# Letting forced background work finish the tasks that already hold buffers, and moving layer 2's units forward, in a four-layer attention kernel

## The chip, the cores and the metric

The kernel runs on one core of a Trainium2 chip. The metric is the time of one execution on the device, in microseconds (us), as the median of several runs.

## The reference

```python
x = x + A(layernorm(x), A_wqkv, A_wo)   # layer 0, sliding window: 0 <= q - k < 256
x = x + B(layernorm(x), B_wqkv, B_wo)   # layer 1, full attention
x = x + A(layernorm(x), A_wqkv, A_wo)   # layer 2, sliding window
x = x + B(layernorm(x), B_wqkv, B_wo)   # layer 3, full attention
# x is 2048 x 640 bf16, 32 heads of 20; attention is not causal in B
# A, B: softmax(q k^T / sqrt(20)) v, then @ wo
```

## The kernel before

The queries are cut into NC = 4 chunks of 512, the heads into G = 8 groups of four. A **unit** is (layer, chunk, group). A full unit of layers 1 and 3 scores 512 queries against all 2048 keys, for four heads; a unit of layers 0 and 2 only needs the window. All units stand in one fixed list, and their score matmuls, exponentials and value matmuls are emitted in this order, one tile of up to 3 x 512 columns at a time. Everything else (layernorm, projections of q, k and v, output products) is **background work**: Python generators, each with a `need`, the index of the unit that wants its result. After each tile `pump` lets the background emit a little, up to a credit. Where a unit's data isn't ready, `require` forces the background on, and no scores are emitted meanwhile; each pass of its loop is called a turn below. Units (1,0,0) to (1,0,2) are halved: part "a" takes the keys of chunks 0 to 2, part "b" those of chunk 3. While layer 0's units and the "a" parts run, every other tile is only 2 x 512 columns wide, and background matmuls have two banks of PSUM (the memory that TensorE writes to); after that they have one. The code is shortened where a comment says so.

```python
def choose(blocked, limit=1 << 30):
    if state["held"] is not None:        # inside an accumulation group
        return state["held"]
    for t in tails:
        if t.wake <= state["tick"]:
            return t
    if not blocked:
        for t in todo:                   # in order of need
            if t.need > limit:
                break
            if t.wake <= state["tick"]:
                return t
    return None

def require(what):
    n = 0
    while what not in ready:
        n += 1                           # ... (an assert)
        t = choose(False, state["unit"] if n < 400 else 1 << 30)
        if t is None:
            state["tick"] += 1
            continue
        state["credit"] = max(state["credit"] - advance(t), -1.0)

cap = {"qa": 3, "ka": 18, "va": 10, "xnT": 5, "kt": 3, "vt": 3, "qt": 4, "ln": 1, "w": 2, "vs": 2}

def room(*tags):
    while any(live[t] >= cap[t] for t in tags):
        yield ("wait", 1)
    for t in tags:
        live[t] += 1

def t_qk_full(key, l, c, g):             # one head group's k and q of a chunk
    # ... (waits for the normalised input)
    wt = yield from take_w(key, l)       # room("w"), then the weights' load
    for n, dst in ((1, k_d[l][:, g, c * C : (c + 1) * C]), (0, q_d[l][:, c, g, :])):
        yield from project(wt, n, xnT[l, c], staged)     # five matmuls, an eviction
        nc.sync.dma_start(out=dst, in_=staging.pop())    # to memory; the unit loads it back
    live["w"] -= 1

# the order of the units (after layer 0's; the rest of layer 3 follows)
units += [Unit(1, 0, g, "a") for g in range(3)]                    # keys of chunks 0 to 2
units += [Unit(1, 0, g, "b" if g < 3 else None) for g in range(G)] # "b": keys of chunk 3
for c in range(1, NC + 1):
    small = deque(Unit(2, c - 1, g) for g in range(G))
    for g in range(G):
        units.append(Unit(1, c, g) if c < NC else Unit(3, 0, g, "a"))
        for _ in range(((0, 0, 1, 1, 2, 2, 2, 0) if c < NC else (0, 0, 2, 3, 3, 0, 0, 0))[g]):
            units.append(small.popleft())

pump(1.2 if cur[0][0].l == 0 else 0.6)   # the credit of one tile
```

The softmax here doesn't subtract the row's maximum and nothing guards it: scores larger than these inputs give would overflow.

Of the kernel before, what the change touches and what calls it, by code (L numbers as in the profile page):

```python
# [23 lines left out]
NC = S // C  # L24
# [7 lines left out]
def kernel(  # L32
# [119 lines left out]
    state = {"tick": 0, "held": None, "credit": 0.0, "early": True, "act": True, "unit": 0}  # L152

    class Task:
# [3 lines left out]

        def __init__(self, name, gen, need):
            self.name, self.gen, self.need, self.wake = name, gen, need, 0  # L160
            Task.count += 1
            self.key = (need, Task.count)

# [9 lines left out]
    def drop(task):  # L173
        (tails if task in tails else todo).remove(task)

    def advance(task):
        try:
            kind, n = next(task.gen)
        except StopIteration:
            drop(task)  # L180
            state["held"] = None
            return 0.0
        state["held"] = task if kind == "hold" else None
        if kind == "wait":
            task.wake = state["tick"] + n
            return 0.0
        return n

    def choose(blocked, limit=1 << 30):
        if state["held"] is not None:  # L190
# [3 lines that stand above are left out]
                return t  # L194
        if not blocked:
            for t in todo:
                if t.need > limit:
                    break
                if t.wake <= state["tick"]:
                    return t  # L200
        return None

    def pump(credit):
        state["credit"] = min(state["credit"] + credit, 1.0)
        while True:
            t = choose(state["credit"] <= 0.0)
            if t is None:
                break
            state["credit"] -= advance(t)
# [17 lines left out]
    def end_early():  # L227
        while mfree[5][0] == 1 << 30:
            advance(state["held"])
        del mfree[5]  # L230
        state["early"] = False
# [4 lines that stand above are left out]
            n += 1  # L236
            assert n < 100000, what
# [5 lines that stand above are left out]
# [5 lines left out]
    def room(*tags):  # L248
        while any(live[t] >= cap[t] for t in tags):
            yield ("wait", 1)  # L250
        for t in tags:
            live[t] += 1

    users = {}

# [35 lines left out]
    def take_w(key, l):  # L291
        yield from room("w")
        order = worder[l]
        i = next(n for n, e in enumerate(order) if e[0] == key)
        if key not in wtiles:
            wtiles[key] = get_w(*order[i][1:])
            if not order[i][3]:
                yield ("wait", 4)
        i = next(n for n, e in enumerate(order) if e[0] == key)
        order.pop(i)  # L300
        wt = wtiles.pop(key)
        if i < len(order) and not any(e[0] in wtiles for e in order):
            wtiles[order[i][0]] = get_w(*order[i][1:])
        return wt
# [35 lines left out]
    def t_ln(l, c):  # L340
        while ("x", l, c) not in ready:
            yield ("wait", 1)
        yield from room("xnT", "ln")
        users[l, c] = 10 if l == 1 else 9
        mv = mvs.pop((l, c))
# [35 lines left out]
    def t_v(l, c, halves):  # L381
# [9 lines left out]
        for i in range(4):  # L391
            if windowed:
                yield from room("va")
                va[c, i] = vap.tile([P, H, VW], BF16, name="va", tag="va")
                nc.gpsimd.memset(va[c, i][:, :, DH : DH + 1], 1.0)
# [176 lines left out]
    for c in range(1, NC + 1):  # L572
        small = deque(Unit(2, c - 1, g) for g in range(G))
        for g in range(G):
            units.append(Unit(1, c, g) if c < NC else Unit(3, 0, g, "a"))
            for _ in range(((0, 0, 1, 1, 2, 2, 2, 0) if c < NC else (0, 0, 2, 3, 3, 0, 0, 0))[g]):
                units.append(small.popleft())
    units += [Unit(3, 0, g, "b") for g in range(G)]
    units += [Unit(3, c, g) for c in range(1, NC) for g in range(G)]
# [304 lines left out]
```

## Time and profile before

| | before |
|---|---|
| median | 2606.18 us (2598.14 to 2611.42, 3 runs) |
| ScalarE busy | 2261.0 us, 87% of the span |
| TensorE busy | 2122.9 us, 81% |
| ScalarE's exponentials waited for scores | 261.8 us, of which one wait 104.7 us and one 35.6 us |
| TensorE's granted clock, mean (share of full speed) | 0.712 |

How to read it: the share of ScalarE is an average over stages. In the filled stages it is busy all the time; what can be won is in the stretches where its exponentials (line 803) wait for score matmuls (line 789). Two waits make up more than half of that.

### The profile page before, as it was taken

What the parts mean: (1) busy time and instruction counts of PE and PEld (TensorE: products, weight loads), DVE (VectorE), ACT (ScalarE), POOL (GpSimd) and SP (SyncE); (2) the same over time, 40 slices, a digit from 0 to 9 for tenths busy, and PEclk for the clock granted to TensorE, in tenths of its full rate; (3) what the DMA queues carried; (4) which work ended last, traced back from release to release, by engine and by line L of the source; (5) the groups of instructions that cost most, each with busy time, mean ns of one, the idle gap of its engine ahead of it and who ended that gap; (6) DMA issues with size and microseconds to landing.
All of it is one profiled execution on the core that took longest, in us unless ns stands there. A gap on an engine that the chain in (4) does not pass through costs nothing.

```text
span 2605.6 us, 37526 instructions
## 1 busy us (share of the span) xinstructions
PE 2122.9 (81%) x15424; PEld 744.8 (29%) x15424; DVE 852.6 (33%) x1925; ACT 2261.0 (87%) x1831; POOL 48.1 (2%) x113
## 2 busy tenths in 40 slices
PE   6889867977888788878888777889887787778777
PEld 3334432322322233322332233323222222222222
DVE  6687833310222233424443343453310011001101
ACT  6778703999999899999999976899999999999996
POOL 2000000000000000000000000000000000000000
PEclk9899987955675669865897668968765565556555
DMA  5112142411211012300222013212310111001100
GB/s 170 61 52 61 50 143 86 127 48 46 59 42 46 16 44 82 104 31 31 72 90 82 1 24 100 88 37 61 111 55 31 31 41 47 31 31 41 47 16 11
DMA packets 92892, 153.03 MB, mean 59 GB/s; under 512 B 8880, under 2 KB 59056, under 8 KB 92720
## 3 DMA queue, kind: packets, MB, share of 16 engines
q1 hardware_dynamic: 92720, 150.64, 18.8%
q8 instruction: 120, 1.97, 0.3%
q14 instruction: 52, 0.43, 0.1%
HBM read 120.46 MB, written 30.15 MB: 58 GB/s over the span
## 4 chain that ended last, share of the span: by engine, by line
ACT 49%; PE 28%; issue 12%; DVE 8%; DMA 2%; SPq 0%; POOL 0%; ACTq 0%; DVEq 0%
ACT pt L803 48%; PE ps L317 10%; PE ps L789 6%; PE ps L481 4%; PE ps L842 4%; PE ps L404 3%; DVE pt L827 2%; DMA wqk<-wqk_d 1%; DVE oT L667 1%; PE ps L368 1%; DVE st L265 1%; DVE qa L265 1%; PE ps L713 1%; DVE x_sb L489 0%; DVE xn L359 0%
## 5 line engine op out<-in xcount | busy, mean ns | idle before, releaser
L803 ACT ACTIVATE pt<-ps 128x1536 bf16<-128x1536 f32 (+1 forms) x1688 | 2194.9, 1562 | 277.7 <-PE ps L789 261.8
L789 PE MATMUL ps<-qt,kt 32*128 32x512 bf16 x4096 | 736.2, 519 | 306.9 <-ACT pt L803 285.0
L842 PE MATMUL ps<-pt,vt 128*21 128x512 bf16 x4096 | 549.3, 522 | 3.7 <-DVE oT L667 1.5
L789 PEld LDWEIGHTS <-kt 32*128 32x128 bf16 x4096 | 209.9, 96 | 793.0 <-issue 770.2
L317 PE MATMUL ps<-xnT,wqk 128*128 128x512 bf16 x1280 | 367.1, 428 | 43.2 <-DMA wqk<-wqk_d 30.6
L827 DVE TENSOR_TENSOR pt<-pt,masks 128x1024 bf16<-128x1024 bf16 (+4 forms) x403 | 239.9, 625 | 242.7 <-ACT pt L803 242.5
L667 DVE CAST oT<-ps 128x512 bf16<-128x512 f32 x117 | 80.2, 685 | 574.8 <-PE ps L842 574.4
L842 PEld LDWEIGHTS <-vt 128*21 128x21 bf16 x4096 | 106.3, 92 | 336.8 <-issue 332.2
L481 PE MATMUL ps<-wop,on 128*128 128x320 bf16 x1024 | 182.6, 327 | 11.1 <-DVE x_sb L489 5.1
L317 PEld LDWEIGHTS <-wqk 128*128 128x128 bf16 x1280 | 120.5, 105 | 223.3 <-issue 107.5
L789 PE MATMUL ps<-qa,ka 32*128 32x256 bf16 (+2 forms) x1408 | 136.5, 322 | 34.0 <-ACT pt L803 30.6
L265 DVE CAST st<-ps 128x512 bf16<-128x512 f32 x119 | 82.3, 691 | 189.9 <-PE ps L317 188.9
L489 DVE TENSOR_TENSOR x_sb<-x_sb,ps 128x320 bf16<-128x320 bf16 x128 | 61.9, 484 | 189.9 <-PE ps L481 187.3
L404 PE MATMUL ps<-wv,xnT 128*128 128x320 bf16 x640 | 114.1, 318 | 10.7 <-DVE vs L265 5.6
L481 PEld LDWEIGHTS <-on 128*128 128x128 bf16 x1024 | 99.0, 105 | 81.4 <-issue 39.4
L717 DVE TENSOR_TENSOR on<-oT,ps 128x512 bf16<-128x512 bf16 x128 | 87.5, 684 | 94.7 <-PE ps L713 94.4
L842 PE MATMUL ps<-pt,va 128*21 128x384 bf16 (+2 forms) x1408 | 89.7, 324 | 18.5 <-DVE oT L667 18.2
L694 DVE RECIPROCAL rz<-ps 128x16 f32<-128x16 f32 x128 | 32.7, 256 | 169.0 <-PE ps L689 159.8
L404 PEld LDWEIGHTS <-xnT 128*128 128x128 bf16 x640 | 60.3, 102 | 53.6 <-issue 30.3
L789 PEld LDWEIGHTS <-ka 32*128 32x128 bf16 x1408 | 40.2, 96 | 122.7 <-issue 115.8
L713 PE MATMUL ps<-rT,spread 32*128 32x128 bf16 x512 | 65.6, 264 | 2.3 <-DVE rT L706 1.5
L368 PE MATMUL ps<-ident,xn 128*128 128x128 bf16 x320 | 35.7, 258 | 31.5 <-DVE xn L359 28.8
(50 smaller groups left out, 647.8 us busy)
## 6 DMA issues: line engine op xcount, KB each, us to landing
wqk<-wqk_d SPq DMA_DIRECT2D x120, 320.0 KB
kt<-k_d SPq DMA_DIRECT2D x53, 512.0 KB
vt<-v_d SPq DMA_DIRECT2D x53, 336.0 KB
qt<-q_d SPq DMA_DIRECT2D x75, 128.0 KB
k_d<-st SPq DMA_DIRECT2D x64, 128.0 KB
q_d<-st SPq DMA_DIRECT2D x64, 128.0 KB
v_d<-vs SPq DMA_DIRECT2D x16, 336.0 KB
wqk_d<-wqk SPq DMA_DIRECT2D x16, 320.0 KB
```

The source lines that it names most:

```text
L265: nc.vector.tensor_copy(out=out_, in_=in_)
L317: nc.tensor.matmul(pq, lhsT=wt[:, n, dc, :], rhs=xt[:, dc, :], start=(dc == 0), stop=(dc == KD - 1),)
L404: nc.tensor.matmul(pv, lhsT=xt[:, dc, i * P : (i + 1) * P], rhs=wv_sb[l % 2][:, dc, h * HD : (h + 1) * HD], start=(dc == 0), stop=(dc == K ...
L481: nc.tensor.matmul(yp, lhsT=on[:, g, qb * P : (qb + 1) * P], rhs=wop[:, g, i * HD : (i + 1) * HD], start=(g == 0), stop=(g == G - 1),)
L489: nc.vector.tensor_tensor(out=xv, in0=xv, in1=yp, op=ALU.add)
L667: nc.vector.tensor_copy(out=oT[:], in_=op)
L713: nc.tensor.matmul(zb[:, qb * P : (qb + 1) * P], lhsT=spread4[:, qb, :], rhs=rT[:], start=True, stop=True,)
L717: nc.vector.tensor_tensor(out=on[:, g, :], in0=oT[:], in1=zb, op=ALU.mult)
L789: nc.tensor.matmul(sp[:, i, col * P : (col + qn) * P], lhsT=u.k(kc, j), rhs=u.q(j, q0, qn), start=True, stop=True,)
L803: nc.scalar.activation(out=pt[:, i:k, b0 * P :], in_=sp[:, i:k, b0 * P :], func=ACT.Exp, scale=SCALE,)
L827: nc.vector.tensor_tensor(out=pt_[:, i:k, b0 * P :], in0=pt_[:, i:k, b0 * P :], in1=mv_, op=ALU.mult,)
L842: nc.tensor.matmul(op[32 * j : 32 * j + VW, q0 * P : (q0 + qn) * P], lhsT=u.v(kc, j), rhs=pt[:, i, col * P : (col + qn) * P], start=(first ...
```

## The change

The intent: a task that has taken a buffer must be able to finish when a forced task needs that buffer, and layer 2's small units should end earlier, so that layer 3's first inputs are made behind layer 1's last units.

```diff
@@ class Task
             self.name, self.gen, self.need, self.wake = name, gen, need, 0
+            self.holds = False
@@ advance
+        state["running"] = task
@@ choose
             for t in todo:
-                if t.need > limit:
-                    break
-                if t.wake <= state["tick"]:
+                if t.wake <= state["tick"] and (t.need <= limit or t.holds):
                     return t
@@ room
             live[t] += 1
+        state["running"].holds = True
@@ order of the units
-            for _ in range(((0, 0, 1, 1, 2, 2, 2, 0) if c < NC else (0, 0, 2, 3, 3, 0, 0, 0))[g]):
+            for _ in range(((0, 0, 2, 2, 2, 2, 0, 0) if c < NC else (0, 0, 2, 3, 3, 0, 0, 0))[g]):
```

The number and the shapes of the instructions stay the same; only their order changes. I call the first four hunks part 1 and the last one part 2. (The changed kernel has one line more, so its exponential is line 804 and its score matmul line 790.)

## The prediction

> **What bounds the kernel now.** I first read the page's share of busy time and the granted clock, then who waited for whom on ScalarE, and then cut the span where ScalarE's work changes its rhythm.
>
> ```profile
> PE 2122.9 (81%) x15424; PEld 744.8 (29%) x15424; DVE 852.6 (33%) x1925; ACT 2261.0 (87%) x1831; POOL 48.1 (2%) x113
> ...
> ACT  6778703999999899999999976899999999999996
> ...
> ACT pt L803 <- PE ps L789: 261.8, 140, 104.7
> ```
>
> ScalarE is the busiest engine (87%) and almost all of its work is the exponential of line 803. The second line, busy tenths in 40 slices, is near 9 except in layer 0 (slices 0 to 4), in slices 5 and 6, and in slices 23 and 24. The third line (who waited for whom: total us, times, longest) says that ScalarE's exponentials waited 261.8 us for score matmuls, and that one single wait was 104.7 us. That is the hole in slices 5 and 6. The busy time by stage, columns PE, PEld, DVE, ACT, POOL, clock, DMA, gives the sizes:
>
> ```profile
> 320.40:425.60 105.20, 69.20 (x290) 29.71 (x290) 37.06 (x61) 0.51 (x2) 0.76 (x2) 0.79 0.43 131
> 425.60:503.70 78.10, 73.40 (x503) 27.21 (x495) 27.75 (x58) 67.84 (x59) 1.82 (x4) 0.84 0.31 92
> 525.50:667.50 142.00, 111.39 (x687) 30.18 (x684) 11.57 (x31) 142.00 (x107) 0.00 (x0) 0.50 0.11 36
> 667.50:760.60 93.10, 79.52 (x566) 29.50 (x566) 26.13 (x61) 87.89 (x66) 1.82 (x6) 0.77 0.20 56
> 1545.30:1583.70 38.40, 20.50 (x99) 9.63 (x98) 11.06 (x24) 2.80 (x3) 1.82 (x4) 0.69 0.36 93
> 1914.80:2115.90 201.10, 155.84 (x965) 42.00 (x964) 15.38 (x42) 201.10 (x152) 0.00 (x0) 0.51 0.11 36
> ```
>
> Three kinds of stage. **Filled**: 525 to 667 and 1915 to 2116, ScalarE busy all the time, 142.0 / 107 = 1.33 us for each tile of 3 x 512 columns; nothing can be gained. **Loaded**: 667 to 760, the same attention with projections and outputs of other chunks mixed in; 93.1 us for 64 such tiles, 1.45 us each. **Holes**: 105.2 us with two exponentials and 38.4 us with three, in which the program issues background work by force and no scores.
>
> What is in the first hole (groups of instructions from 319 to 427 us: busy, mean ns, idle before), and what of it is on the chain that ended last (start, length):
>
> ```profile
> L317 PE MATMUL ps<-xnT,wqk 128*128 128x512 bf16 x200 | 58.0, 459 | 28.6 <-DMA wqk<-wqk_d 28.6
> ...
> L404 PE MATMUL ps<-wv,xnT 128*128 128x320 bf16 x70 | 10.5, 298 | 1.0 <-DVE vs L265 0.8
> ...
> 326.00 3.36 PE ps L317 x15
> ...
> 412.04 2.82 DMA wqk<-wqk_d
> 414.91 4.46 PE ps L317 x10
> ...
> 421.45 3.45 DMA qt<-q_d
> ```
>
> The last four lines are the chain. 200 matmuls of line 317 are 40 projections, q or k of one head group. Layer 1's first unit needs only two of them, and they are the last: the x10 at 414.91. The rest is work for units up to 240 us later. The scheduler explains it. I followed the scheduling code of the kernel before step by step (it runs when the program is built). At unit (1,0,0,"a") `require` wants the task ("qk",1,2,0). It asks for one of two weight slots, but ("qk",1,1,1) and ("qk",1,1,2) hold both, and their need (units 33 and 34) is above the limit 32, so `choose` breaks out. The loop turns idly until its 400th turn, drops the limit, and then runs every pending task in order of need, ("qk",1,2,0) last: 934 turns. No other `require` in the program gets beyond 114 turns.
>
> **What the Trainium skill says.** "ScalarE: Activation LUTs", section What ACT_TABLE_LOAD costs, gives an ACTIVATE 186 ns + 0.833 ns per element, about 93 ns of it overlapped back to back: an estimate of 1466 - 93 = 1373 ns for 1536. The trace has 1.33 us, so the filled stages are at ScalarE's limit. "TensorE: Matmul & The Clock Gate", section Step-by-step: what each phase is for, says that matmuls stay in program order and only weight loads are pulled ahead; the trace agrees: no score matmul of the next unit comes before the forced projections end. The same page, What's actually happening, says that the clock is halved by default and released by activity: filled stages were granted 0.50, the loaded one 0.77. So background work partly pays for itself by a faster clock. "Perfetto Trace Analysis", Optimization Strategy, advises interleaving regimes with different bounds, which is what the change aims at.
>
> **The change part by part.**
>
> *Part 1, holders are finished.* At that same `require`, the two holders are now run. What remains in the hole: the last layernorm transpose and four value groups (to 323.9 in the trace), tails (to 325.6), the one projection that ("qk",1,1,1) lacks and two of ("qk",1,1,2) (the x15 at 326.00, to 329.4), the weights of ("qk",1,2,0) (issued about 328.4, some 3.5 us as in the chain, to 332), its two projections (4.5 us at the slow end as at 414.91, to 336), eviction and write out (2 us, as from 419.4 to 421.45), and the loads (3.45 us). The first exponential would come at about 342 instead of 425.6. **Hole: 105 to 22 us, minus 83.**
>
> *What it pushes back.* 34 of the 40 projections (17 tasks) and 10 of the 14 value groups become background work of layer 1's first chunk. The program counts 1.1 for a projection and 0.7 for a group: 34 x 1.1 + 10 x 0.7 = 44 units of credit. A tile gets 0.6, so this is 74 tiles' worth. Does it fit? From (1,0,0,"a") to (1,0,7) there are about 181 tiles, 108 credits; the work already there (output of layer 0's last chunk 9, its layernorm 1.6, values 5.6, 8 tasks of 2.2, tails 5) is 39, so 83 in all. By deadlines: 25 of 34 credits before unit (1,0,0,"b"), 36 of 43 before (1,0,3), 55 of 56 before (1,0,4), 65 of 69 and 74 of 82 after that. It fits, tightly at (1,0,4). The cost of hidden work: loaded minus filled is 1.45 - 1.33 = 0.12 us per tile, 0.2 us per credit. 44 x 0.2 = 9 us; with forced remainders at (1,0,4), **plus 12.**
>
> *Part 2, layer 2's units earlier.* In chunks 1 to 3 the eight small units now end before g = 6, not before g = 7. The second hole (1545 to 1583.7) is the forced chain from out(2,2), layernorm, values (8 groups at 2.07 us each in the chain, because with one bank a group waits for its eviction) to the projections of (3,2,0), then 5 us of loads. Before, that chain had 21 tiles of (1,3,7) after the last small unit; now it has 42. What was forced is 1.1 + 1.6 + 5.6 + 2.2 = 10.5 credits; the extra 21 tiles give 12.6. But with one bank and the waits in the tasks I count some 49 tile steps from the start of the last small unit to the end of (3,2,0), against 46 to its deadline, so a projection or two and the load latency should stay: about 10 us of hole. **38 to 10, minus 28; hidden cost 10.5 x 0.2, plus 2.**
>
> *What part 2 costs.* Unit (2,c-1,1) is wanted 21 tiles earlier. Before, in chunks 2 and 3 the last projection of (2,c-1,0) was just forced, 6 steps. But that came late because tasks of layer 3 held weight slots, and these now run a unit earlier. I allow one projection pair in each chunk and some holders finished early in other forced stretches: **plus 4.**
>
> The exponentials themselves are unchanged, and from 1884 us on the kernel is filled; nothing changes there. Sum: -83 + 12 - 28 + 2 + 4 = -93; 2606 - 93 = 2513, say **2515 us**.
>
> **The rivals.** (a) *The work comes back exposed.* The pushed back projections could miss deadlines and be forced unit by unit, each with a weight wait (28.6 us of waits in the hole for 6 loads). For it: 55 of 56 credits at (1,0,4). Against: all those forced now find their holders finished, and 525 to 667 is now idle in background. If half came back exposed, some 30 us more: 2545. (b) *Another blocked require.* The value slots (two) are counted without the new mark, so two later value tasks could block ("v",1,3,0) and the 400-turn release would fire again, with perhaps 60 us of hole: 2575. Against: an earlier value task with a lower need goes first and the holders run while it waits. I give it 5%. (c) *Part 2 only moves its hole*: the chain is still late or layer 2 is forced at g = 2: 20 to 25 us less gain, 2538. For it: the 46 against 49 steps. (d) *Better than I say*: loaded tiles at a warm clock cost nothing more, and the second hole vanishes: 2490.
>
> **Range and chances.** Part 1's gain is sure in kind (70 to 85 net is most of it) and by itself exceeds 2% (52 us). (d) sets the low end, 2490; (a) or (c) sets the high end, 2548. Within 2% needs (a) beyond half or (b): 0.09. Slower needs a new hole as large as the old: 0.01. Faster: 0.90.
>
> **What would show it.** Right: ScalarE's longest wait falls from 104.7 to about 22 us; from the first unit of layer 1 to 330 us later the rhythm is 1.4 to 1.5 us per tile and the clock above 0.7 where it was 0.50; the wait of 35.6 us before (3,0,0,"a") falls to 10 or less; the last 690 us keep their length. Wrong: several new waits of 5 to 10 us at the starts of units in layer 1's first chunk (a), a wait above 50 us (b), or waits of ScalarE at units (2,1,0) and (2,2,0) (c).

## The result, and the profile after

| | before | after |
|---|---|---|
| median | 2607.43 us (4 runs) | 2525.13 us (2514.65 to 2530.09, 4 runs) |
| ratio | | 0.9684, 95% interval 0.9643 to 0.9725 |
| ScalarE waited for scores | 261.8 us | 167.3 us |
| longest such waits | 104.7 and 35.6 us | 20.7, 8.1 and 6.2 us |

A ratio is the mean time of one kernel's runs over that of the other's of the same rounds, so it is not quite the ratio of the medians. The profiled run of the changed kernel (2514.65 us) was the fastest of its four. All outputs are right.

From the page and from who waited for whom on ScalarE (total us, times, longest), changed kernel:

```profile
PE 2049.3 (82%) x15313; PEld 730.0 (29%) x15424; DVE 851.9 (34%) x1925; ACT 2264.0 (90%) x1831; POOL 48.2 (2%) x113
...
ACT  6778866899998999899999988899999999999995
...
ACT pt L804 <- PE ps L790: 167.3, 154, 20.7
```

ScalarE does the same work (2264 us, before 2261) in a shorter span. In slices 5, 6 and 23, 24 of 40 the busy tenths had fallen to 0, 3 and 7, 6; they are now 6, 6 and 9, 9.

ScalarE runs its exponentials in program order, so the start of each unit is the start of the exponential with that number. Cutting the span at such starts gives the table on which everything below rests (us of the profiled runs; the two parts alone are experiments, below):

| stage | before | after | part 1 alone | part 2 alone |
|---|---|---|---|---|
| to the first exponential of layer 1 | 425.6 | 337.4 | 343.1 | 425.5 |
| (of it the last wait) | 104.7 | 20.7 | 20.8 | 105.1 |
| layer 1, chunk 0 | 241.9 | 274.8 | 271.5 | 241.6 |
| layer 1, chunks 1 and 2, with layer 2 | 587.3 | 585.4 | 587.0 | 585.2 |
| layer 1, chunk 3, with layer 2 | 328.9 | 300.1 | 334.8 | 300.4 |
| (of it the last wait) | 35.6 | 6.2 | 37.8 | 6.4 |
| layer 3, chunk 0, with layer 2 | 300.7 | 295.3 | 301.8 | 303.9 |
| rest of layer 3 | 721.2 | 719.9 | 721.1 | 721.2 |

Four differences: the first hole, minus 84.0; layer 1's first chunk, **plus 32.9**; the chunk with the second hole, minus 28.8; the chunks between, minus 1.9. They add up to minus 81.8, and the medians differ by 82.3. The profiled runs differ by 92.7, because this run was also 4.2 us early at the first hole and 5.4 us faster in layer 3's first chunk; other runs with the same program there (343.1, and 301.8 or 303.9) were not, so I don't count these two. (The run at 0.8 in the first chunk, below, has the same program in layer 3's first chunk and took 300.6 us there.)

The busy time by stage (PE, PEld, DVE, ACT, POOL, clock, DMA share, GB/s). First layer 1's first chunk of the kernel before, whose parts the prediction shows:

```profile
425.60:667.50 241.90, 202.25 (x1316) 63.38 (x1309) 46.44 (x105) 231.31 (x180) 1.82 (x4) 0.64 0.21 65
```

then the changed kernel: the first hole, two stretches of the same chunk (the "a" and the "b" parts) and at the end the whole of it, the last unit before layer 3, layer 3's first chunk, the filled end.

```profile
316.20:337.40 21.20, 11.79 (x62) 5.98 (x64) 7.89 (x16) 0.54 (x3) 0.38 (x1) 0.84 0.46 145
337.40:421.60 84.20, 73.87 (x522) 27.99 (x526) 31.44 (x64) 67.44 (x59) 1.92 (x4) 0.91 0.34 94
421.60:458.90 37.30, 27.10 (x157) 9.03 (x155) 10.02 (x21) 22.31 (x16) 0.39 (x1) 0.76 0.35 110
...
1460.60:1497.70 37.10, 28.62 (x209) 11.08 (x207) 11.65 (x27) 29.17 (x23) 1.82 (x4) 0.77 0.37 96
1497.70:1793.00 295.30, 247.15 (x2010) 92.47 (x2026) 130.05 (x271) 275.85 (x203) 3.64 (x10) 0.86 0.27 80
1793.00:2486.60 693.60, 550.10 (x3486) 159.43 (x3483) 65.31 (x170) 688.40 (x513) 0.00 (x0) 0.54 0.11 35
...
337.40:612.20 274.80, 225.66 (x1518) 77.63 (x1535) 75.06 (x150) 233.69 (x180) 2.30 (x5) 0.82 0.31 96
```

The reader is to see that in layer 1's first chunk ScalarE's work is the same (231 and 234 us), TensorE's rises from 202 to 226 us (the projections that left the hole; a few matmul records of this trace are missing), and the clock from 0.64 to 0.82; and that 421.6 to 458.9 is a bad stretch: 16 exponentials in 37.3 us, 2.3 us each where a filled stage has 1.33. These are the three "b" units.

What happens there: the timeline of the changed kernel around the start of unit (1,0,1,"b") (start, length, engine, line, what; in brackets the idle time before and what ended it).

```profile
431.83 0.32 SPq L464 DMA_DIRECT2D k_d<-st  x1
431.86 1.24 PE L318 MATMUL ps<-xnT,wqk 128*128 128x512 bf16 x5 [0.78 <-DVE st L266]
433.03 0.38 PE L790 MATMUL ps<-qt,kt 32*128 32x512 bf16 x1
433.14 0.69 DVE L266 CAST st<-ps 128x512 bf16<-128x512 f32 x1 [1.33 <-PE ps L318]
433.86 0.32 SPq L464 DMA_DIRECT2D q_d<-st  x1
...
435.20 0.42 SPq L608 DMA_DIRECT2D qt<-q_d  x1
437.44 0.61 PE L790 MATMUL ps<-qt,kt 32*128 32x512 bf16 x2 [4.02 <-DMA qt<-q_d]
...
438.15 2.79 ACT L804 ACTIVATE pt<-ps 128x1536 bf16<-128x1536 f32 x2 [8.12 <-PE ps L790]
```

A task of two projections, k and then q of chunk 3 (2.5 us of matmuls), is late; but the unit can only start after k was stored (431.83) and loaded back (`kt`, in the queue after `vt` at 434.23), and so ScalarE waits 8.1 us. The q in between isn't wanted here: the `qt` that is loaded at 435.20 is chunk 0's, made long before. But the task counts as ready only after both, so some 2.0 us of the wait (k's store at 431.83 to q's at 433.86) go to a result that no unit wants yet. No run tried to part the two. The same happens at the other two "b" units, with 4.5 and 2.5 us. Here are the waits from 418 to 460 us, changed kernel:

```profile
ACT pt L804 <- PE ps L790: 19.5, 9, 8.1
...
PE ps L790 <- DMA qt<-q_d: 11.2, 3, 4.4
```

A fourth wait, 5.6 us at 383, is a background projection whose weights had not landed. From the chain and the waits between 374 and 392 us, changed kernel:

```profile
371.68 8.13 DMA wqk<-wqk_d
...
PE ps L318 <- DMA wqk<-wqk_d: 3.6, 1, 3.6
```

It held up the score matmuls behind it on TensorE, as the program order of matmuls that the prediction quotes would have it. In the whole chunk ScalarE's idle time rose from 10.6 us (241.9 less 231.3 busy) to 41.1 us (274.8 less 233.7); these four waits are 20.7 us of it, the others about 2 us each or less.

The scheduling code, followed alone, says the same in counts. The `require` before layer 1 takes 64 turns instead of 934, the one before layer 3 takes 6 instead of 114; new ones appear at the "b" units, with 1, 13 and 3 turns.

### The profile page after: what moved, and what is told of

The parts are those of the page before. It is cut to its first block, busy times and chain, and to the rows that moved or that the text cites. A ratio compares the mean times of both kernels' runs of the same rounds, so it can differ in the third digit from the quotient of the medians.

```text
span 2512.9 us, 37403 instructions
## 1 busy us (share of the span) xinstructions
PE 2049.3 (82%) x15313; PEld 730.0 (29%) x15424; DVE 851.9 (34%) x1925; ACT 2264.0 (90%) x1831; POOL 48.2 (2%) x113
## 4 chain that ended last, share of the span: by engine, by line
ACT 47%; PE 28%; issue 13%; DVE 9%; DMA 2%; SPq 0%; ACTq 0%; POOL 0%; DVEq 0%
ACT pt L804 46%; PE ps L318 9%; PE ps L790 6%; PE ps L843 4%; PE ps L482 4%; PE ps L405 4%; DVE pt L828 3%; DMA wqk<-wqk_d 1%; DVE oT L668 1%; PE ps L369 1%; DVE st L266 1%; DMA qt<-q_d 1%; DVE on L718 1%; DVE qa L266 1%; DVE x_sb L490 1%
## 5 line engine op out<-in xcount | busy, mean ns | idle before, releaser
L804 ACT ACTIVATE pt<-ps 128x1536 bf16<-128x1536 f32 (+1 forms) x1688 | 2198.2, 1537 | 184.6 <-PE ps L790 167.3
L790 PE MATMUL ps<-qt,kt 32*128 32x512 bf16 x4096 | 713.9, 504 | 302.4 <-ACT pt L804 268.8
L843 PE MATMUL ps<-pt,vt 128*21 128x512 bf16 x4096 | 533.8, 507 | 6.0 <-DVE oT L668 3.6
L790 PEld LDWEIGHTS <-kt 32*128 32x128 bf16 x4096 | 204.2, 95 | 771.5 <-issue 738.3
L318 PE MATMUL ps<-xnT,wqk 128*128 128x512 bf16 x1169 | 345.0, 413 | 34.8 <-DMA wqk<-wqk_d 7.8
L828 DVE TENSOR_TENSOR pt<-pt,masks 128x1024 bf16<-128x1024 bf16 (+5 forms) x403 | 239.7, 624 | 215.6 <-ACT pt L804 215.3
L790 PE MATMUL ps<-qa,ka 32*128 32x384 bf16 (+2 forms) x1408 | 132.5, 318 | 31.3 <-ACT pt L804 28.9
L266 DVE CAST st<-ps 128x512 bf16<-128x512 f32 x119 | 82.3, 691 | 208.5 <-PE ps L318 208.1
```

Of the source, the lines that this page charges most:

```text
L266: nc.vector.tensor_copy(out=out_, in_=in_)
L318: nc.tensor.matmul(pq, lhsT=wt[:, n, dc, :], rhs=xt[:, dc, :], start=(dc == 0), stop=(dc == KD - 1),)
L790: nc.tensor.matmul(sp[:, i, col * P : (col + qn) * P], lhsT=u.k(kc, j), rhs=u.q(j, q0, qn), start=True, stop=True,)
L804: nc.scalar.activation(out=pt[:, i:k, b0 * P :], in_=sp[:, i:k, b0 * P :], func=ACT.Exp, scale=SCALE,)
L828: nc.vector.tensor_tensor(out=pt_[:, i:k, b0 * P :], in0=pt_[:, i:k, b0 * P :], in1=mv_, op=ALU.mult,)
L843: nc.tensor.matmul(op[32 * j : 32 * j + VW, q0 * P : (q0 + qn) * P], lhsT=u.v(kc, j), rhs=pt[:, i, col * P : (col + qn) * P], start=(first ...
```

## The experiments

Nine kernels in three groups; the kernel before ran beside each group (medians 2604.19, 2605.28 and 2602.36 us). My theory: the two parts act in two different holes and add up, and the 33 us that the first part gives back are partly avoidable lateness. Rivals are in the expectations.

### Part 1 alone

```diff
 (the changed kernel)
-((0, 0, 2, 2, 2, 2, 0, 0) if c < NC
+((0, 0, 1, 1, 2, 2, 2, 0) if c < NC
```

> The changed kernel with the old order of layer 2's units: part 1 alone. Theory (the two parts act in two different holes and add up): the wait of 105 us before layer 1 becomes about 21 us, the first chunk of layer 1 takes 33 us longer as in the changed kernel, the wait of 36 us before layer 3 stays. 2607 - 84 + 33 = about 2556 us, ratio 0.980. Rival (the parts need each other: work pushed back by part 1 is only absorbed because layer 2 ends earlier): the stretch from layer 1's second chunk to layer 3 gets longer than before, over 916 us, and the time is above 2575.

Measured: 2557.17 us (2553.29 to 2560.98, 4 runs), ratio 0.9816 (0.9786 to 0.9846). The stages are in the table above: the first hole has gone, the first chunk is 29.6 us longer, the second hole (37.8 us) stays. The stretch from chunk 1 to layer 3 is 921.8 us against 916.2, so the rival's sign is there, but with 6 us, of which 2.2 are in the wait itself; the total is what the theory said.

### Part 2 alone

```diff
 (the kernel before)
-((0, 0, 1, 1, 2, 2, 2, 0) if c < NC
+((0, 0, 2, 2, 2, 2, 0, 0) if c < NC
```

> The kernel before with the new order of layer 2's units and nothing else: part 2 alone. Theory (adding): the wait of 105 us stays, the wait of 36 us before layer 3 becomes about 6 us, the stretch from layer 1's second chunk to layer 3 shortens from 916 to about 885 us: about 2576 us, ratio 0.988. Rival (the second hole only moves): the wait reappears before layer 2's first units or inside layer 3, time within 10 us of 2607.

Measured: 2577.77 us (2572.88 to 2579.51, 4 runs), ratio 0.9889 (0.9854 to 0.9923). The first hole stays (105.1 us), the second falls to 6.4 us and appears nowhere else: chunks 1 and 2 take 585.2 us, not more than before. Longest wait of ScalarE with part 1 alone, and with part 2 alone:

```profile
ACT pt L804 <- PE ps L790: 208.4, 160, 37.8
```

```profile
ACT pt L803 <- PE ps L789: 229.9, 144, 105.1
```

Each part takes away its own hole and leaves the other's. The losses from 1, 0.0184 and 0.0111, add up to 0.0295; both parts together gave 0.0316, with an interval of 0.0275 to 0.0357. They add within the noise.

### Three weight slots instead of two

```diff
 (the kernel before)
-wqkp = pool("wqkp", 4)
+wqkp = pool("wqkp", 5)
-xtp = pool("xtp", 5)          # room for the fifth; never more than 3 are held
+xtp = pool("xtp", 4)
-cap: "xnT": 5, "w": 2
+cap: "xnT": 4, "w": 3
```

> The kernel before with three weight slots instead of two (one weight buffer more, one of the normalised inputs' buffers, of which it never holds more than three, less). Theory (the hole comes from holders above the limit, however many slots there are; a third slot is held too): the single wait before layer 1 stays near 105 us, certainly above 90; time within 15 us of 2607. Rival (two slots are too few): the wait falls below 40 us and the time to about 2550.

Measured: 2581.07 us, one run of unknown state. The hole is still there, as the theory says: the third slot is held as well, and `require` turns 815 times. But the wait is 74.9 us, below the 90 that I had set. Both of my numbers missed. The stage and the groups within it, three slots (the prediction shows two slots: 105.2 us, 459 ns for a matmul of line 317, 28.6 us waited for weights, clock 0.79):

```profile
325.00:399.90 74.90, 56.53 (x275) 25.88 (x274) 35.22 (x59) 0.00 (x2) 0.77 (x2) 0.94 0.59 177
...
L317 PE MATMUL ps<-xnT,wqk 128*128 128x512 bf16 x200 | 49.7, 406 | 10.5 <-DMA wqk<-wqk_d 10.5
```

The same 200 matmuls waited 18 us less for weights, and TensorE was granted 0.94 of its clock instead of 0.79. So a third slot changed how fast the forced work ran, not whether it was forced. A single run is no measure of the gain in time.

### Five halved units: chunk 3's keys wanted later

```diff
 (the changed kernel)
-units += [Unit(1, 0, g, "a") for g in range(3)]
-units += [Unit(1, 0, g, "b" if g < 3 else None) for g in range(G)]
+units += [Unit(1, 0, g, "a") for g in range(5)]
+units += [Unit(1, 0, g, "b" if g < 5 else None) for g in range(G)]
```

> The changed kernel with five instead of three of layer 1's first units split into an a part (chunks 0 to 2) and a b part (chunk 3), so that chunk 3's keys are wanted some 40 tiles later. Theory (about 15 of the 33 us by which the first chunk of layer 1 got longer are three forced projections with their store and load at the b parts, because chunk 3's chain is just late): the waits of 4.5, 8.1 and 2.5 us at the b parts go, the first chunk takes 255 to 262 us instead of 275, time about 2510. Rival (the hidden work itself costs more than 0.2 us per unit of credit, wherever it is): the first chunk stays at 270 to 278 us, with the loss spread over all tiles, time 2520 to 2530.

Measured: 2502.37 us (2494.71 to 2504.15, 4 runs), ratio 0.9600 (0.9569 to 0.9631), so it also beats the changed kernel (0.9643 at the low end of its interval). Layer 1's first chunk, five halved units:

```profile
341.80:594.70 252.90, 221.52 (x1541) 76.55 (x1540) 76.52 (x152) 233.65 (x187) 2.21 (x5) 0.84 0.35 105
```

252.9 us instead of 274.8, with the same projections hidden in it, and no wait above 2 us at a "b" unit; both the stage and the time came out below my theory. The chunk is now 11.0 us over the kernel before, with one wait for weights of 5.2 us still in it. Of the 21.9 us gained, 15.1 are the three waits at the "b" units; most of the others are shorter waits. That all 21.9 were lateness is not shown: with two more units halved, the background also keeps its second bank of PSUM for two units longer and gets six more tiles (1837 instructions on ScalarE instead of 1831). No run separates these from the deadline; the next one only gives a hint.

### A faster background in the first chunk

```diff
 (the changed kernel)
-pump(1.2 if cur[0][0].l == 0 else 0.6)
+pump(1.2 if cur[0][0].l == 0 else 0.8 if (cur[0][0].l, cur[0][0].c) == (1, 0) else 0.6)
```

> The changed kernel with background work at 0.8 instead of 0.6 units of credit per tile, in layer 1's first chunk only. Theory (the three forced projections at the b parts are late by little; a faster background removes them as the later deadline did): no wait above 3 us at the b parts, first chunk 255 to 262 us instead of 275, time 2508 to 2514. Rival (TensorE has no room for a faster background there: it was busy 74 of 84 us in the a parts at a clock of 0.91): the tiles get longer instead, first chunk 268 us or more, time above 2518.

Measured: 2513.74 us (2510.82 to 2520.36, 4 runs), ratio 0.9652 (0.9616 to 0.9689). Its "a" and "b" parts:

```profile
341.30:430.60 89.30, 83.75 (x586) 32.35 (x586) 38.85 (x76) 69.13 (x58) 2.30 (x5) 0.96 0.42 120
430.60:454.70 24.10, 21.04 (x159) 7.86 (x157) 9.64 (x21) 21.91 (x16) 0.00 (x0) 0.91 0.63 205
```

The waits at the "b" units have gone, and those units take 24.1 us instead of 37.3; but the "a" units take 89.3 us instead of 84.2 (in which the first of the three waits, 4.5 us, is counted), so that the chunk takes 266.9 us, above my 255 to 262. The time is as the theory said, and a part of the rival is true: where the rate is higher, the tiles get longer. The total is not separated from the changed kernel's (the intervals overlap); that the waits have gone is shown. By the scheduling code nothing in this chunk is late here, as with five halves: no `require` turns in it. And yet it is 25.0 us over the kernel before, and there 11.0. So "nothing late" doesn't by itself bring the price down to 11 us. The two kernels differ in the rate and in the units with a second bank; which of these it is, is not shown.

### Five halved units at 0.7 and at 0.8 everywhere

```diff
 (five halved units)
-pump(1.2 if cur[0][0].l == 0 else 0.6)
+pump(1.2 if cur[0][0].l == 0 else 0.7)     # the second run: 0.8
```

> Five halved units and 0.7 units of credit per tile in layers 1 to 3 (layer 0's units keep 1.2). Theory (what is left of the second hole, 6 us, and the 5 us before unit (2,3,0) are forced ends of chains that are late by a few tiles; 0.7 instead of 0.6 makes them early): both waits below 2 us, time about 2490, 10 to 14 us under the five halves alone. Rival (background work costs time in proportion to the rate wherever it lies): no gain over the five halves, 2500 to 2510.

> As the run before with 0.8. Theory: once no task is late, a higher rate gains nothing more; the same work is put into fewer tiles, each of which is longer: within 6 us of the run with 0.7. If TensorE becomes the bound in the loaded tiles, 5 to 20 us slower than with 0.7.

Measured: 2523.14 us (2520.20 to 2529.84, 4 runs), ratio 0.9689 (0.9658 to 0.9720), with 0.7; 2532.93 us (2523.99 to 2534.31, 4 runs), ratio 0.9725 (0.9692 to 0.9757), with 0.8. My theory fell. The waits before layer 3 and before unit (2,3,0), 6.6 and 4.8 us, did fall to about 2 us or less; yet the kernel lost 20 us against the five halves alone, clear of the noise. With 0.8 it was 9.8 us slower still, with overlapping intervals. The stages with 0.7 (layer 1's chunk 0, chunks 1 and 2, chunk 3, layer 3's chunk 0), and then the last of them with 0.6:

```profile
337.60:598.00 260.40, 227.55 (x1541) 77.24 (x1539) 76.41 (x152) 235.25 (x187) 2.21 (x5) 0.81 0.34 102
598.00:1187.80 589.80, 498.87 (x3731) 177.14 (x3727) 215.92 (x487) 543.75 (x423) 7.28 (x20) 0.72 0.18 55
1187.80:1490.90 303.10, 252.58 (x1959) 90.67 (x1958) 115.66 (x250) 278.09 (x204) 3.63 (x10) 0.76 0.19 55
1490.90:1799.40 308.50, 266.51 (x2026) 95.16 (x2024) 129.44 (x270) 277.96 (x204) 3.63 (x10) 0.78 0.26 76
```

```profile
1478.20:1773.40 295.20, 248.49 (x2031) 92.72 (x2027) 130.12 (x271) 275.94 (x204) 3.66 (x10) 0.86 0.27 80
```

Every loaded stage got longer (with 0.6: 252.9, 583.4, 300.1, 295.2), with nearly the same ScalarE work and a lower granted clock. The last stage is no safe sign: at 0.6 it took from 295.2 to 303.9 us in nine kernels' profiles, and with 0.8 everywhere 300.9. The first two are: with 0.8 they took 264.1 and 595.2 us, at clocks of 0.78 and 0.72. Closing a wait of 6 us by making all background faster costs more than the wait.

### A slower background in the middle

```diff
 (five halved units)
-pump(1.2 if ... else 0.6)               # the condition as before
+pump(1.2 if ... else 0.5 if (cur[0][0].l, cur[0][0].c) in ((1, 1), (1, 2), (2, 0), (2, 1)) else 0.6)
```

> Five halved units, and background work at 0.5 instead of 0.6 units of credit per tile in the middle chunks (layer 1's chunks 1 and 2 with layer 2's units between them), where no task comes late at that rate either. The rates 0.7 and 0.8 cost 20 and 30 us although they left no forced wait. If the price of hidden work rises with its rate (several projections in one tile overflow the 1.33 us that ScalarE needs for it), the slower rate gains: the two chunks take 571 us or less together instead of 583, time 2488 to 2497. If the price depends on the amount alone, the same as the five halves: 2498 to 2506.

Measured: 2496.77 us (2490.26 to 2500.64, 4 runs), ratio 0.9577 (0.9539 to 0.9614). The time lies in the band of "the price rises with the rate", but the stage does not: chunks 1 and 2 take 582.1 us against 583.4, not 571. Between 0.5 and 0.6 the rate makes no visible difference in the very stage that was changed, and the intervals of this run and of the five halves overlap. So the loss at 0.7 is not simply proportional to the rate. Why it starts there stays open; the runs show only that the clock is lower and the tiles longer.

### All eight units halved

```diff
 (as five halved units, with range(8) and g < 8)
```

> The changed kernel with all eight of layer 1's first units halved, so chunk 3's keys are wanted some 60 tiles later still than with five. Theory (only lateness costs, and with five halves nothing is late any more): no further gain, within 6 us of the 2502 of five halves. Rival (more distance to the deadline keeps helping): below 2494.

Measured: 2497.57 us (2494.18 to 2503.04, 4 runs), ratio 0.9590 (0.9558 to 0.9622), within 6 us of the five halves: more distance to the deadline gains nothing once nothing is late. Five halves, eight halves and the slower middle cannot be told apart by these runs; all three are 2502 us or less, about 1% below the changed kernel.

## Why the prediction was right or wrong

The predicted time was 2515 us, the measured one 2525 us, within the range. That it came so near is partly luck: one term was 20.9 us worse than predicted, and the others together 9.7 us better. By its steps:

- **First hole, 105 to 22 us: right.** 104.7 to 20.7 us, in both kernels with part 1. The blocked `require` is what makes the hole: it stays with the new order alone (105.1 us) and with a third slot (74.9 us), and goes when holders may finish.
- **The work pushed back, plus 12: the mis-sized term.** It measured plus 32.9 us (29.6 with part 1 alone). The step that failed is the count by deadlines, "25 of 34 credits before unit (1,0,0,"b")", and from it "It fits, tightly at (1,0,4)". I compared sums of credit. But the tasks of chunk 3 are a chain (tail, output, layernorm, values, projections) with waits between them, and the last projections of that chain ended just after their units. The lateness was small, 1 to 13 turns, but each late projection also exposes its store and its load: waits of 4.5, 8.1 and 2.5 us, 15.1 in all, where the prediction had 3 us for forced remainders. Another 5.6 us came from weights that landed late, and most of the rest lies in shorter waits. With five halved units the term is 11.0 us, near the 9 us that I had worked out for the hidden work; with the faster background, where nothing is late either, it is 25.0. So how much of the 32.9 is the price of hidden work alone stays open. (The prediction's window also held one projection from before the hole: 39, not 40, were in it. The 34 pushed back are right.) Rival (a) had named this; I gave it too little weight and the wrong place, (1,0,4) instead of the "b" units.
- **Second hole, 38 to 10, with 2 for hidden work: right.** The chunk became 28.8 us shorter, its last wait went from 35.6 to 6.2 us. The count of 49 steps against 46 was right in sign: one `require` of 6 turns was left, with its loads.
- **Cost of part 2, plus 4: not there.** Chunks 1 and 2 became 1.9 us shorter, and no wait arose at units (2,1,0) and (2,2,0): the forced ends of 6 turns there, where ScalarE had waited 0.5 and 0.8 us, are gone in the new order. Rival (c) did not happen.
- **Sum:** predicted minus 93; measured minus 81.8 in these stages and minus 82.3 by medians. The pushed back work cost 20.9 us more than I had it; the first hole, the second hole with its hidden work, and part 2's cost came out 1.0, 2.8 and 5.9 us better.
- **Rival (b)**, a second blocked `require`: did not happen; the longest wait after the first hole is 8.1 us. **Rival (d)**, a second hole that vanishes and free loaded tiles: did not happen here; the wait can be closed, but by a rate that cost more.
- **The signs** given in the prediction came as said for the right case, with one of the wrong case: waits of up to 8 us at the starts of units in layer 1's first chunk, and with them a rhythm of 2.3 us per tile in the "b" units, not 1.4 to 1.5.

## What to carry to other kernels

When a scheduler limits forced work by priority, tasks of lower priority that already hold a scarce buffer must be exempt, or the forced task waits for them and an escape rule dumps everything at once; here a third buffer (one run) only changed how long the dump took. When work is moved out of a hole into hidden slots, check the deadlines along each chain with its store and load, not only the sum of work. And where a few tasks are late by little, move their deadline rather than speed up all the background.

## What the Trainium skill lacked or had wrong

- "TensorE: Matmul & The Clock Gate" ties the release of the clock to activity in a window of some microseconds, but doesn't say how much of a window must be busy. In the filled stage of the kernel before TensorE was busy 111.4 of 142.0 us (78%) and was granted 0.50 on average; in a loaded stage, 79.5 of 93.1 us (85%), it was granted 0.77.
- "ScalarE: Activation LUTs" gives an overlap of about 93 ns between back-to-back ACTIVATEs. Here 1466 ns by its formula became one exponential every 1.33 us, so some 136 ns overlapped in this stream (or 120 ns, taken from the 1.45 us that a lone exponential took in the changed kernel's trace).
- No page gives the price of a store to memory followed by a load of the same data, on which the main miss rests. Here it was 5.1 us from the issue of k's store (431.83) to the first weight load from `kt` (436.92), for 128 KB, and 5.9 us in the first hole of the changed kernel (330.47 to 336.39, 128 KB stored and 384 KB loaded), both with the projection of q in between. From the issue of the load alone it was 2.2 and 3.5 us. "DMA: Bandwidth & Descriptors" has a fixed cost of about 2.0 us for one DMA in its section on the SWDGE path, and these DMAs are issued from the sync engine.
